# A transformer block planned by its own scheduler: fillers by a running count, later loads of the last weights, other shares of the softmax, and a direct key projection

## The chip, the cores and the metric

The kernel runs on one core of a Trainium2 chip. The core has TensorE for matrix products (PE in the profile, its weight loads PEld), VectorE (DVE), ScalarE (ACT), GpSimd (POOL) and SyncE (SP), whose queue issues nearly all transfers here. Matrix products land in PSUM, eight banks of 128 partitions by 512 floats. The metric is the device time of one execution in microseconds. The time before is 812.66 us, the median of three runs of 808.64 to 812.86.

## The reference

One block of a transformer with adaptive layer norm: 2048 tokens of 640 features, 32 heads of 20, and a gated feed-forward layer of width 1536 without a nonlinearity. All inputs are bf16.

```python
mod = silu(c) @ w_mod                      # six vectors of 640: sa, ca, ga, sb, cb, gb
h = layernorm(x) * (1 + ca) + sa
q, k, v = split(h @ wqkv)                  # 32 heads of 20
p = softmax(q @ k.T * 20 ** -0.5)          # 32 x 2048 x 2048
x = x + ga * ((p @ v) @ wo)
h = layernorm(x) * (1 + cb) + sb
x = x + gb * (((h @ w_gate) * (h @ w_up)) @ w_down)
```

## The kernel before

**How it is made.** The kernel file is a planner. It makes tasks (one or a few instructions each, with an engine, an assumed duration, dependencies, a priority and sometimes a gate), plays them through a model of the core, engine by engine, and then writes out each engine's instructions in the order that came out, with semaphore waits where one engine needs another. So the order on each queue is fixed when the program is built, and a changed number in the planner can move every instruction. At run time each engine goes through its list in order and waits where its data is late.

**Tiling.** The heads form eight sets of four; the four heads of a set sit in the four 32-row strips of the array, so that their products run side by side. The queries are cut into six chunks (`CHUNKS`): two of 512 tokens and four of 256, numbered 0 to 5. An item is one chunk and one head set, 48 in all; the last one is halved. A unit is 512 columns of scores: one head, 128 keys by 512 queries, or 256 keys by 256 queries. An item has 64 units with 512 queries, 32 with 256.

**The softmax.** Scores (line 1502) come out with keys on the partitions. Most units go in pairs to ScalarE, whose exponential (1539) writes a bf16 tile of 1024 columns into a ring `PP`; two pairs of PSUM banks take turns. The other units go in quads of four to VectorE. It builds the exponential from the bits of a scaled score: one instruction per unit turns it into an integer (1563), two passes over the quad's 2048 columns take the mantissa and the exponent (1595, 1603), and one product (1600 on VectorE, or four pieces at 1615 on GpSimd, whichever is free first in the plan) makes the first of two terms. The product with the values (2165) takes a ScalarE unit once and a quad's unit twice, once per term. `QUADS` says how many quads each head set of each chunk has. There are 104 quads, so 816 exponentials are left for ScalarE.

**Around it.** Layer norm, the projections of keys, queries and values, and the modulation vectors are made at the start and during chunk 0. A key projection of 512 tokens is either direct (`kq_round`, matmuls at 1148: one head set per round, already spread over the four strips, evicted straight into the key tile `KT`), or packed (`packed_round`, 1212: 128 features per round, evicted to `KPA`, written to memory, and read back into the strips, four reads per head set, issued at 1271). `K_DIRECT` makes head set 0 direct for all four blocks of 512 tokens; `K_ALL` lists blocks in which all sets are direct, and is empty.

When an item's products are done, its PSUM bank is transposed (1695), divided by the softmax's sum (1702, on GpSimd), transposed again into `OcT` (1711), and moved by a few small transfers into `Ocp` (1723), four or five per item. When the eight items of a chunk are there, its suffix follows: output projection with `wo` (`op`), second layer norm, transposes into h2T (1866), gate and up products with weights streamed from memory (1907), their product, and the down projection with `wd`. The suffix of one chunk is spread over the scores of the next as optional work for TensorE. The last chunk's suffix runs behind all scores, with full-width matmuls (948; 952 is the four-strip form). Its weights are loaded into buffers `stx` that take the place of dead query tiles; ten of its twelve pairs of loads go there, of which the first wait for the last scores of chunk 4 (`qdead`), and the rest for chunk 3's down projection (`first`). The others go through three rotating buffers `stg`.

**How TensorE's order is chosen.** `pick_pe` takes, at each free moment of TensorE in the plan: the next pair of scores if its banks and inputs are ready; quad units that are late; nothing, if the next scores are about to be ready (`HOLD`); optional work, if TensorE's recent activity is under `FILL_MIN`; a filler, if it is under `FILL_HARD` (0: never); a batch of value products; optional work; and last a filler, if activity is under `FILL_MIN` and nothing else is there. A filler (2498) is four matmuls of the identity into a spare bank, and its result isn't used. Activity is counted as array area over the last `HAM_W` = 3413.3 ns; the planner counts cold windows on a fixed grid and doubles its durations behind one (`roll`). `STAGE` sets such numbers anew at given items.

A load's landing in the plan is its issue, a rate, a latency, and, past 60 us, `DMA_MARGIN`.

## Time and profile before

| | |
|---|---|
| runs | 812.86, 808.64, 812.66 us |
| profiled execution | 814.7 us, span 812.9 us |
| mean granted clock of TensorE | 0.991 |
| PE busy, instructions | 796.0 us, 14867 |
| DVE busy | 685.9 us, 1337 |
| ACT busy | 767.0 us, 851 |
| POOL busy | 360.6 us, 374 |

Engine busy times are unions of instruction spans. A group's row has the line, engine and operation, what it writes and reads, the shape and count, then its busy time, the mean duration in ns, and the idle time of the engine ahead of it with what ended most of that. In the rows of a windows view each stretch has its length, each engine's busy time and count, the clock that TensorE was granted (1.00 is full speed), the share of the DMA engines, and GB/s. Chunk 0's exponentials begin at 17 us; the later chunks' begin at about 214, 401, 497, 592 and 684 us, and the last exponential ends at 780 us.

### The profile page before, as it was taken

What the parts mean: (1) busy time and instruction counts of PE and PEld (TensorE: products, weight loads), DVE (VectorE), ACT (ScalarE), POOL (GpSimd) and SP (SyncE); (2) the same over time, 40 slices, a digit from 0 to 9 for tenths busy, and PEclk for the clock granted to TensorE, in tenths of its full rate; (3) what the DMA queues carried; (4) which work ended last, traced back from release to release, by engine and by line L of the source; (5) the groups of instructions that cost most, each with busy time, mean ns of one, the idle gap of its engine ahead of it and who ended that gap; (6) DMA issues with size and microseconds to landing.
All of it is one profiled execution on the core that took longest, in us unless ns stands there. A gap on an engine that the chain in (4) does not pass through costs nothing.

```text
span 812.9 us, 34131 instructions
## 1 busy us (share of the span) xinstructions
PE 796.0 (98%) x14867; PEld 345.3 (42%) x14867; DVE 685.9 (84%) x1337; ACT 767.0 (94%) x851; POOL 360.6 (44%) x374
## 2 busy tenths in 40 slices
PE   8999999999999999999999999999999999999998
PEld 4434424332233222233343334445555555554567
DVE  7888868899999799998988878976798989799564
ACT  6899999999999799999999999999999999999941
POOL 2346344563374343444446334453546555652200
PEclk9999999999999699999999999999999999999999
DMA  9743222213241242201300232100432054444410
GB/s 298 238 121 81 59 58 65 58 33 109 73 103 34 82 114 62 49 4 46 71 17 11 49 79 56 38 23 23 97 86 54 26 118 102 98 95 97 95 36 18
DMA packets 136387, 60.49 MB, mean 74 GB/s; under 512 B 100703, under 2 KB 136239, under 8 KB 136239
## 3 DMA queue, kind: packets, MB, share of 16 engines
q1 hardware_dynamic: 135311, 57.16, 27.4%
q8 instruction: 118, 1.93, 1.1%
q10 hardware_dynamic: 928, 1.15, 0.4%
q14 instruction: 30, 0.25, 0.1%
HBM read 46.70 MB, written 8.99 MB: 69 GB/s over the span
## 4 chain that ended last, share of the span: by engine, by line
PE 49%; ACT 40%; issue 6%; DVE 3%; DMA 1%; SPq 0%; ACTq 0%; DVEq 0%
ACT PP L1539 40%; PE ps_all L1502 17%; PE ps_all L952 13%; PE ps_all L2165 11%; PE ps_all L1212 3%; PE ps_all L948 3%; DMA wm<-in_w_mod_dram 1%; DVE DB L1563 1%; PE ps_all L1109 1%; DVE DSS L1595 1%; PE ps_all L1866 1%; PE ps_all L1148 1%; DVE DSS L1603 0%; PE ps_all L2498 0%; DVE KPA L1221 0%
## 5 line engine op out<-in xcount | busy, mean ns | idle before, releaser
L1539 ACT ACTIVATE PP<-ps_all 128x1024 bf16<-128x1024 f32 x816 | 751.0, 1157 | 7.4 <-PE ps_all L1502 6.5
L1615 POOL TENSOR_TENSOR DSS<-DB,DSS 128x512 bf16<-128x512 bf16 x260 | 295.5, 1155 | 325.1 <-DVE DSS L1603 273.4
L1502 PE MATMUL ps_all<-QT,KT 32*128 32x256 bf16 (+2 forms) x3136 | 324.0, 308 | 9.5 <-ACT PP L1539 6.1
L1563 DVE TENSOR_SCALAR DB<-ps_all 128x512 int16<-128x512 f32 x416 | 277.4, 682 | 55.1 <-PE ps_all L1502 52.8
L1502 PEld LDWEIGHTS ps_all<-QT,KT 32*128 32x128 bf16 x3136 | 89.7, 92 | 239.4 <-ACT PP L1539 202.9
L2165 PE MATMUL ps_all<-PP,Vf 128*32 128x256 bf16 (+2 forms) x2520 | 165.8, 313 | 0.8 <-DVE DB L1563 0.4
L952 PE MATMUL ps_all<-h2T,stg 128*32 128x256 bf16 (+2 forms) x2272 | 122.8, 303 | 0.2 <-DVE DB L1563 0.2
L2165 PEld LDWEIGHTS ps_all<-PP,Vf 128*32 128x32 bf16 (+1 forms) x2520 | 49.6, 94 | 83.1 <-issue 76.0
L2165 PE MATMUL ps_all<-DSS,Vf 128*32 128x256 bf16 (+1 forms) x1232 | 84.6, 317 | 0.1
L1595 DVE TENSOR_SCALAR DSS<-DB 128x2048 int16<-128x2048 int16 x104 | 74.2, 713 | 0.5
L1603 DVE TENSOR_SCALAR DSS<-DB 128x2048 int16<-128x2048 int16 x104 | 72.8, 700 | 0.6 <-PE ps_all L2165 0.6
L952 PEld LDWEIGHTS ps_all<-h2T,stg 128*32 128x32 bf16 x2272 | 50.9, 96 | 28.1 <-issue 21.4
L952 PE MATMUL ps_all<-wd,hprod 128*32 128x320 bf16 (+1 forms) x1348 | 62.4, 281 | 0.0
L1702 POOL TENSOR_TENSOR OTn<-OT,invT 128x256 bf16<-128x256 f32 (+1 forms) x47 | 38.5, 820 | 53.0 <-DVE invT L1700 53.0
L1600 DVE TENSOR_TENSOR DSS<-DB,DSS 128x2048 bf16<-128x2048 bf16 x39 | 49.3, 1265 | 0.1
L2165 PEld LDWEIGHTS ps_all<-DSS,Vf 128*32 128x32 bf16 (+1 forms) x1232 | 29.5, 95 | 24.6 <-issue 14.2
L952 PEld LDWEIGHTS ps_all<-wd,hprod 128*32 128x32 bf16 x1348 | 31.1, 96 | 16.0 <-issue 10.3
L952 PE MATMUL ps_all<-wV,hT 128*32 128x160 bf16 x1280 | 37.3, 234 | 0.5 <-DVE hT L1117 0.2
L1695 DVE STREAM_TRANSPOSE OT<-ps_all 128x256 f32<-128x256 f32 (+2 forms) x49 | 25.7, 524 | 13.2 <-PE ps_all L2165 12.9
L1212 PE MATMUL ps_all<-hT,wq 128*32 128x512 bf16 x375 | 33.2, 397 | 0.0
L1212 PE MATMUL ps_all<-hT,wk 128*32 128x512 bf16 (+1 forms) x360 | 32.8, 382 | 0.2 <-DVE Vf L1301 0.2
L952 PE MATMUL ps_all<-wo,Ocp 128*32 128x320 bf16 (+1 forms) x664 | 30.7, 280 | 0.3
(131 smaller groups left out, 524.6 us busy)
## 6 DMA issues: line engine op xcount, KB each, us to landing
stg<-in_B_w_gate_dram SPq DMA_DIRECT2D x62, 160.0 KB
stg<-in_B_w_up_dram SPq DMA_DIRECT2D x62, 160.0 KB
KT<-k_rows SPq DMA_DIRECT2D x112, 32.0 KB
wm<-in_w_mod_dram SPq DMA_DIRECT2D x3, 800.0 KB
x<-in_A_x_dram SPq DMA_DIRECT2D x7, 320.0 KB
k_rows<-KPA SPq DMA_DIRECT2D x16, 128.0 KB
QT<-q_rows SPq DMA_DIRECT2D x32, 64.0 KB
wd<-in_B_w_down_dram SPq DMA_DIRECT2D x1, 1920.0 KB
```

The lines of the kernel that those rows point to most:

```text
L952: return lambda e, b: e.matmul(ps[32 * x:32 * x + 32, b, c0 + o:c0 + o + w], lhs()[:, 32 * x:32 * x + 32], rhs() if w == n else rhs()[:, o ...
L1212: f = [lambda e, b_, k=k, x=x: e.matmul(ps[x:x + min(32, w - x), b_, :], wx[:, k, r0 + x:r0 + min(x + 32, w)], hT[tc][:, k, :], tile_posit ...
L1502: ems.append(lambda e, i=i, kt=kt: e.matmul(dstf()[:, i * u.n:(i + 1) * u.n], KT[32 * u.s:32 * u.s + 32, u.j, kt * 128:(kt + 1) * 128], QT ...
L1539: return e.activation(PPs[g % 2][:, cellp["p"], 0:nu * 512], ps[:, b0:b0 + nu, :].rearrange("p b c -> p (b c)"), AFT.Exp, scale=ESCALE)
L1563: return e.tensor_scalar(DBl[st_["slot"]][:, x * 512:(x + 1) * 512], bank(cell["b"]), EBIAS, 0.0, op0=ALU.add, op1=ALU.max)
L1595: return e.tensor_scalar(DSl[st_["ss"][0]][:, :], DBl[st_["slot"]][:, :], 0x7F, 0x3F00, op0=ALU.bitwise_and, op1=ALU.bitwise_or)
L1600: return e.tensor_tensor(d, DBl[st_["slot"]][:, :].bitcast(BF16), d, ALU.mult)
L1603: return e.tensor_scalar(DSl[st_["ss"][1]][:, :], DBl[st_["slot"]][:, :], 0x7F80, 2, op0=ALU.bitwise_and, op1=ALU.bitwise_or)
L1615: return e.tensor_tensor(d, DBl[st_["slot"]][:, x * w:x * w + w].bitcast(BF16), d, ALU.mult)
L1695: t1 = Task("dve", n * 1.1 + 70, lambda e: e.transpose(OT[:, 0:n], ps[:, item_info[it]["bank"], 0:n].rearrange("p (b q r) -> p b r q", q=3 ...
L1702: f3 = lambda e: e.tensor_tensor(OTn[:, 0:n].rearrange("p (b c r) -> p b r c", c=32, r=2), OT[:, 0:n].rearrange("p (b r c) -> p b r c", c= ...
L2165: ems.append(lambda e, i=i, kt=kt, stt=stt, stp=stp: e.matmul(ps[32 * s:32 * s + mc, bk, 0:u.n], Vf[:, (kt * H + 4 * u.j + s) * VW:(kt * H ...
```

## The change

The planner's numbers and rules change at these places.

- `roll` and `activity` keep four windows, staggered by a quarter, in place of one. Any of them under `HAM_MIN` makes the plan cold; only the first clears it.
- `FILL_HARD` is 3000 in place of 0, and the filler's test stands ahead of the optional work at low activity.
- The loads of the last chunk's weights into `stx` wait, beside what they waited for, for the transfers of chunk 4's attention outputs into `Ocp` (`oc_ready`). The plan's size of these and of the streamed weight loads (each 160 KB) goes from `2 * 128 * KD * 128 * 2` bytes to `int(STG_B * 128 * KD * 128 * 2)` with `STG_B` = 0.95, that is from 327,680 to 155,648.
- `QUADS` of chunks 2 and 3.
- `K_ALL` is `(0,)`: head sets 1 to 7 of the first 512 keys are projected by direct rounds; the five packed rounds of that block go.
- `END3` is 1: the division for the last head set of chunks 0 to 4 goes from GpSimd to VectorE.
- `DMA_MARGIN` is 500 in place of 1000.
- The transposes into h2T wait for the gate and up products that last read that buffer (for `first` in chunk 4); their evictions did so before.
- `STAGE` has other numbers for most items.

```diff
-DMA_MARGIN = 1000.0
+DMA_MARGIN = 500.0
...
     def roll(self, t):
-        w = int(t // HAM_W)
-        while self.ham_w < w:
-            self.cold = self.ham_act < HAM_MIN
-            if self.cold:
-                self.ncold += 1
-            self.ham_act = 0.0
-            self.ham_w += 1
+        for i in range(4):
+            w = int((t - i * HAM_W / 4) // HAM_W)
+            while self.ham_w[i] < w:
+                low = self.ham_act[i] < HAM_MIN
+                if low:
+                    self.ncold += 1
+                if i == 0 or low:
+                    self.cold = low
+                self.ham_act[i] = 0.0
+                self.ham_w[i] += 1
...
-QUADS = (..., (2, 1, 2, 1, 2, 1, 2, 1), (2, 1, 2, 1, 2, 1, 2, 1), (2, 2, 1, 2, 2, 2, 1, 2), ...)
+QUADS = (..., (2, 2, 1, 2, 2, 2, 1, 2), (2, 2, 1, 2, 2, 2, 1, 2), (2, 2, 1, 2, 2, 2, 1, 2), ...)
...
-K_ALL = ()
+K_ALL = (0,)
...
-FILL_HARD = 0.0
+FILL_HARD = 3000.0
...
-ENDP, END3, P_POW = 0.4, 0, -1.0
+STG_B = 0.95
+ENDP, END3, P_POW = 0.4, 1, -1.0
...
-            r = Round(mms, list(t_xn2), after, pr(True), gate=gate(n), name=f"h2T{ci}.{k}")
+            r = Round(mms, t_xn2 + (first if alt else bd.get("h2T", [])), after, pr(True), gate=gate(n),
+                      name=f"h2T{ci}.{k}")
...
-                t = dma("sp", 2 * 128 * KD * 128 * 2, f, sfx_done["qdead"] if use_x and fc < nsq else first if use_x else kp_use if ci == 0 else [], prio=16 + ci + .01 * fc,
+                t = dma("sp", int(STG_B * 128 * KD * 128 * 2), f,
+                        (sfx_done["qdead"] if fc < nsq else first) + oc_ready[(NC - 2, CHUNKS[-2][1] // 128 - 1)] if use_x else
+                        kp_use if ci == 0 else [], prio=16 + ci + .01 * fc,
...
+        if sc.recent(t) < FILL_HARD and t > 20000 and do_fill(t):
+            return True
         if sc.recent(t) < FILL_MIN and ring() >= RINGLOW and pick_x(t, True):
             return True
-        if sc.recent(t) < FILL_HARD and t > 20000 and do_fill(t):
-            return True
```

73 lines of the change are left out of this document (40 added, 33 removed).

## The prediction

> **What bounds the kernel now.** I read the page's first parts, then its costliest groups.
>
> ```profile
> span 812.9 us, 34131 instructions
> PE 796.0 (98%) x14867; PEld 345.3 (42%) x14867; DVE 685.9 (84%) x1337; ACT 767.0 (94%) x851; POOL 360.6 (44%) x374
> ...
> ACT  6899999999999799999999999999999999999941
> ...
> PEclk9999999999999699999999999999999999999999
> ...
> L1539 ACT ACTIVATE PP<-ps_all 128x1024 bf16<-128x1024 f32 x816 | 751.0, 1157 | 7.4 <-PE ps_all L1502 6.5
> ```
>
> ACT's row is full from the third slice to the third last, but for one; TensorE's 98% is partly the modelled ends of pipelined matmuls. Nearly all of ACT is one line, the exponential over two score units: 751.0 / 816 = 0.920 us each. So the span is three stretches: a head until ACT is full, 816 exponentials end to end, and a tail. The windows view and the groups of one stretch say how full:
>
> ```profile
> 20.00:100.00 80.00, 77.91 (x1414) 32.90 (x1416) 69.59 (x152) 76.31 (x85) 37.35 (x45) 1.00 0.45 128
> 260.00:280.00 20.00, 19.42 (x153) 4.67 (x153) 15.16 (x26) 15.54 (x17) 8.29 (x8) 0.66 0.06 16
> 300.00:320.00 20.00, 19.91 (x282) 5.95 (x274) 20.00 (x37) 20.00 (x23) 8.01 (x8) 1.00 0.24 55
> 395.00:490.00 95.00, 93.39 (x1788) 38.11 (x1788) 79.96 (x148) 94.94 (x104) 44.20 (x48) 1.00 0.16 38
> 490.00:587.00 97.00, 96.80 (x2146) 46.56 (x2142) 76.69 (x144) 97.00 (x107) 44.00 (x46) 1.00 0.20 49
> 587.00:680.00 93.00, 92.20 (x2253) 49.27 (x2252) 83.44 (x166) 92.88 (x102) 50.49 (x51) 1.00 0.31 71
> ...
> L1539 ACT ACTIVATE PP<-ps_all 128x1024 bf16<-128x1024 f32 x210 | 193.3, 1132 | 0.1
> ```
>
> Columns: stretch, length, busy time of PE, its weight loads, DVE, ACT and POOL (each with its count), granted clock, DMA share, GB/s. ACT lacks 80 - 76.31 = 3.7 us before 100 us, lacks 4.5 us in the slice where the clock is 0.66, and lacks nothing in chunks 2 to 4 (395 to 680). The last row is ACT's group from 400 to 592: 0.1 us idle. There only fewer exponentials can help, and retuned stage settings cannot.
>
> **The change part by part.**
>
> *More quads on VectorE.* The tuple for chunks 2 and 3 goes from 2,1,2,1,2,1,2,1 (12) to 2,2,1,2,2,2,1,2 (14): four sets gain a quad, two lose one. So the net is four quads in all, though the change is named for six: 104 become 108. A quad is four units and an exponential takes two: 8 exponentials fewer, 8 x 0.920 = 7.4 us off ACT. VectorE pays, by these rows:
>
> ```profile
> L1563 DVE TENSOR_SCALAR DB<-ps_all 128x512 int16<-128x512 f32 x416 | 277.4, 682 | 55.1 <-PE ps_all L1502 52.8
> ...
> L1603 DVE TENSOR_SCALAR DSS<-DB 128x2048 int16<-128x2048 int16 x104 | 72.8, 700 | 0.6 <-PE ps_all L2165 0.6
> L1600 DVE TENSOR_TENSOR DSS<-DB,DSS 128x2048 bf16<-128x2048 bf16 x39 | 49.3, 1265 | 0.1
> L1615 POOL TENSOR_TENSOR DSS<-DB,DSS 128x512 bf16<-128x512 bf16 x260 | 295.5, 1155 | 325.1 <-DVE DSS L1603 273.4
> ```
>
> Per quad 4 x 0.682 + 2 x 0.700 (the two passes have one shape) = 4.1 us, and the product either on VectorE (1.27, 5.4 in all) or on POOL (4 x 1.155 = 4.6; POOL is half idle). Chunk 3: 76.7 + 2 x 5.4 = 87.5 of 97 - 3.7. Chunk 2 is tight: 80.0 + 10.8 = 90.8 of 95 - 3.7 = 91.3. Chunk 4 already has the new pattern, with ACT at 92.88 of 93, and from 300 to 320 VectorE is busy 20.00 of 20 with ACT still full. So I book VectorE's extra 17 to 22 us at nothing; if chunk 2 overflows, its share of the gain is lost (a rival below). TensorE's second product pass for 16 units has the same cover.
>
> *Fillers by a running count.* The planner now keeps four staggered 3.4 us windows, and puts in a filler as soon as its count of the last window is under 3000 (a full window is 3413 ns x 2.37, about 8090), ahead of optional work. What this is about:
>
> ```profile
> 263.00:264.00 1.00, 1.00 (x6) 0.18 (x6) 1.00 (x3) 1.00 (x2) 0.56 (x1) 0.50 0.03 8
> ...
> 259.60:263.00 3.40, 2.82 (x25) 1.05 (x23) 3.40 (x7) 3.40 (x5) 1.92 (x2) 1.00 0.13 32
> 200.20:203.60 3.40, 2.30 (x28) 0.64 (x26) 3.40 (x6) 2.86 (x4) 0.18 (x1) 1.00 0.52 154
> 306.00:309.40 3.40, 3.40 (x57) 1.15 (x53) 3.40 (x9) 3.40 (x5) 0.00 (x0) 1.00 0.10 25
> L1539 ACT ACTIVATE PP<-ps_all 128x1024 bf16<-128x1024 f32 x11 | 11.1, 1056 | 4.4 <-PE ps_all L1502 4.4
> L2498 PE MATMUL ps_all<-ident x128: 379/379/391, 219.5 to 742.8; 128*32 128x512 bf16 x128
> ```
>
> The granted clock halves at 263, and by the slice's 0.66 stays there some 20 x 0.34 / 0.5 = 13.6 us, after 3.4 us with 25 matmuls where an ordinary stretch has 57. The stretch at 200 was as thin (28) and kept its clock: it depends on how the count falls. While the clock is low the exponentials wait for scores (group of 262.9 to 276.7). The price: 17 exponentials in that 20 us slice instead of 23, 6 x 0.92 = 5.5 us; the idle time alone is 4.5. I take 5.5, as each lone exponential also runs longer than its 0.92 in a stream. Without it this execution would be 814.7 - 5.5 = 809.2, close to the lowest timed run, 808.64. A filler is four matmuls of 0.38 us side by side; before had 32. Costs are in the cover row below.
>
> [...]
>
> *Last weights behind the attention outputs.* These rows are from the timeline, tiles, groups by form, DMA issues, and the chain in order of time.
>
> ```profile
> 687.27 0.31 DVE L1711 STREAM_TRANSPOSE OcT<-OTn 128x128 f32<-128x128 f32 x1
> 692.56 2.99 SPq L1723 DMA_DIRECT2D Ocp<-OcT  x4
> 702.37 0.53 PE L952 MATMUL ps_all<-wo,Ocp 128*32 128x320 bf16 x12
> L952 PE MATMUL ps_all<-h2Tt,stg x544: 219/272/283, 725.5 to 774.9; 128*32 128x256 bf16 x140, 128*32 128x128 bf16 x42
> L952 PE MATMUL ps_all<-wd,hprodt x192: 298/299/310, 781.8 to 789.9; 128*32 128x320 bf16 x192
> L952 PE MATMUL ps_all<-wd,hprodt 128*32 128x320 bf16 x192 | 7.3, 300 | 0.0
> x<-in_A_x_dram ACTq DMA_DIRECT2D x1, 320.0 KB, 2.9
> 783.49 1.35 DVE L1856 TENSOR_SCALAR h2Tc<-ps_all,mcol 128x128 bf16<-128x128 bf16 x5
> 775.95 2.26 ACT PP L1539 x2
> ...
> 783.56 4.05 PE ps_all L952 x116
> ...
> 790.15 20.07 PE ps_all L948 x300
> ```
>
> Chunk 4's last output is transposed by 687.6 but issued at 692.6, behind weight loads on SP, and first used at 702.4. Issued at once, with 3.0 us for the four issues and 2.9 to land (the one transfer whose landing the page times, an estimate here), they would be there at 693.5: the projection could start 8.9 us sooner. What it feeds ends late: all 48 down-projection steps of chunk 4 (192 matmuls, 8 us) run after the last exponential and push chunk 5's final 20.07 us to 790.15. Gate and up of chunk 4 take 725.5 to 774.9, 49.4 us for 12 x 10 steps of 256 columns; 8.9 us is 18% of that, 5,530 columns, or 36% of the down projection's 48 x 320 = 15,360: 0.36 x 7.3 us busy = 2.6 us off the tail from this alone. Ends: nothing, and 790.15 - (783.49 + 1.35) = 5.3 us, when chunk 5's first half is ready and nothing is left over. The moved loads have until 790 and start near 693: covered.
>
> *First 512 keys projected direct.* K_ALL = (0,) is the first token block, all head sets 1 to 7 (the name says head set 0). Five packed rounds become seven direct ones:
>
> ```profile
> L1212 PE MATMUL ps_all<-hT,wk 128*32 128x512 bf16 (+1 forms) x360 | 32.8, 382 | 0.2 <-DVE Vf L1301 0.2
> ```
>
> Matmuls: 140 for 90, or +50 x 32.8 / 360 = +4.6 us of TensorE at the spread-out price; two evictions more (0.68 each); 28 reads (7 sets by 4 strips) and 6 writes go from SP. It lies in the head, where ACT lacks 3.7 us: ends -3.7 and +4.6, and I take 0.
>
> *The planner's idea of loads.* For the streamed weights the plan's size goes from 327,680 bytes, twice the true 160 KB, to 155,648, and the margin from 1.0 to 0.5 us. At the plan's 240 bytes per ns and 0.0015 ns per byte that is a landing 0.72 + 0.26 + 0.5 = 1.5 us sooner, 3.1 us after the issue instead of 4.6. Nothing in the chip changes but the order: rounds may be placed sooner.
>
> ```profile
> SPq L1907 <- PE ps_all L952: 95.9, 46, 4.1
> stg<-in_B_w_gate_dram SPq DMA_DIRECT2D x62, 160.0 KB
> 678.64 0.53 SPq L1907 DMA_DIRECT2D stg<-in_B_w_up_dram  x1
> 680.50:681.00 0.50, 0.50 (x26) 0.29 (x14) 0.50 (x1) 0.50 (x2) 0.00 (x0) 1.00 0.75 167
> ...
> PEld ps_all L973 <- DMA wm<-in_w_mod_dram: 1.7, 2, 1.1
> ...
> PEld ps_all L1502 <- ACT PP L1539: 202.9, 642, 1.4
> ```
>
> SP waits for TensorE to free a buffer (95.9 us), so landing time is in each buffer's cycle. The pair whose second load is issued at 678.64 has ended its traffic by 681, 2.4 us later, so 3.1 still holds in a quiet queue, and no PE row waits for a transfer but one at the start. Chunk 4 turns its three buffers (12 - 3) / 3 = 3 times: up to 4.4 us sooner, which I add to the 8.9: 13.3 / 49.4 = 27%, 8,270 columns, 54% of 15,360, and 0.54 x 7.3 = 3.9 us off the tail in place of 2.6, still inside 0 to 5.3.
>
> *The rest.* Five normalisations go from POOL to VectorE, the transposes of h2T carry one wait more (for a buffer that their evictions waited for already), and some forty stage settings change: beside a full ACT, 0. Fillers too: the score loads wait 642 times for ACT, 0.32 us on average (last row), so a filler of 0.38 us costs at most some hundredths; with that cover gone, 0.38 each.
>
> **Sum**, against this execution's own 814.7 (span 812.9): 814.7 - 7.4 - 5.5 - 3.9 = 797.9. The median of the runs is 812.66 and the lowest 808.64; two runs near 812.7 look like this one and the lowest like one whose clock held, from which the sum is 808.64 - 11.3 = 797.3. I predict 798.
>
> **The rivals.** (1) *The clock still falls once.* For: the stretch at 200 shows that a thin stretch is decided by where it falls, and the planner's count is not the chip's. Against: the new count looks at every moment, and four phases are kept. 814.7 - 7.4 - 3.9 = 803.4. (2) *The quads do not pay.* For: chunk 2's 90.8 of 91.3 us, and 55.1 us in which VectorE waited for scores, which it cannot make up. Then late quads hold the products back and ACT waits instead: no 7.4, 814.7 - 5.5 - 3.9 = 805.3; with the tail unmoved as well, 809.2. Against: chunk 4 and 300 to 320. (3) *Slower: TensorE stalls on weights that the plan counts too early.* Its queue is in order, so behind a gate or up round that waits stand the next scores, and ACT behind them. In a dense stretch the plan now moves a 160 KB load in 0.65 us; the half microsecond from 680.5 moved 167 GB/s, 0.98 us for as much. Price: up to 1.5 us for each of the 62 streamed pairs, 93 us at worst. It decides from (816.7 - 798) / 1.5 = 13 pairs fully late. Against: no such wait now, and the 0.7 us between 2.4 and 3.1. At some 20 pairs, 798 + 30 = 828.
>
> **How the numbers follow.** A measurement of this kernel can tell about 0.5%, 4 us, from no change: 808.6 to 816.7. Chances: forecast 0.60, rival 1 0.15, rival 2 0.13, rival 3 0.12. Faster: 0.60 + 0.15 + half of rival 2 = 0.81; same: the other half and the mild part of rival 3, 0.09; slower 0.10. Range: low end with the full tail and the head's idle time gained, 814.7 - 7.4 - 5.5 - 5.3 - 3.7 = 793; high end with the clock fall kept, no tail gain and the direct keys' full price nearly, 814.7 - 7.4 + 3.7 = 811.
>
> **What would show it.** Exponentials x808 at 0.92; no stretch under 1.00 in the clock row; ACT full from 100 us on; VectorE's group L1563 x432; chunk 4's first projection near 693 and part of its down projection ahead of the last exponential; 28 key reads fewer. Wrong: ACT waiting for scores in chunk 2, PE rows that wait for DMA, or a clock under 1.00.

## The result and the profile after

The changed kernel takes 807.97 us, the median of 20 runs (803.90 to 815.22). The kernel before took 811.37 us beside it, also over 20 runs (808.19 to 817.06). The ratio is 0.9954, with a 95% interval of 0.9934 to 0.9974. So the change is worth about 3.7 us. Here and below the medians and ranges hold every run, and the ratios leave out three runs (one of e2_space, two of e7_q3) that were over 1.5% above the fastest of their kernel. I had forecast 798 us, and a change of 16.8 us in the profiled execution (814.7 to 797.9). The profiled execution of the changed kernel took 810.71 us, 4.0 less.

The lines of the file have moved: 1539 is now 1550 (exponentials), 1502 is 1513 (scores), 1563 is 1574, 1595 is 1606, 1603 is 1614, 1600 is 1611, 1615 is 1626 (quads), 1702 is 1713 (the division), 1907 is 1919 (streamed weights), 952 and 948 are 963 and 959. These lines of the page after answer to those shown of before:

```profile
span 808.9 us, 34210 instructions
...
PE 791.2 (98%) x14913; PEld 346.7 (43%) x14913; DVE 700.8 (87%) x1368; ACT 761.1 (94%) x843; POOL 375.6 (46%) x385
...
PEclk9999999998999999999999999999999999999999
...
L1550 ACT ACTIVATE PP<-ps_all 128x1024 bf16<-128x1024 f32 x808 | 745.4, 1109 | 11.6 <-PE ps_all L1513 10.6
...
L1574 DVE TENSOR_SCALAR DB<-ps_all 128x512 int16<-128x512 f32 x432 | 288.4, 683 | 46.4 <-PE ps_all L1513 43.7
...
KT<-k_rows SPq DMA_DIRECT2D x84, 32.0 KB, 1.7
```

The counted things came as forecast: 808 exponentials at 745.4 / 808 = 0.92 us, 432 quad units on VectorE, 84 key reads in place of 112. But ScalarE's exponentials now stand idle for 11.6 us, ended by scores; before it was 7.4. The stretches, from the starts of the exponentials at each chunk's border, say where. The third column is the mended kernel e6_end_wait of the experiments below, which has the changed kernel's order of instructions but for ten loads:

| us | before | after | e6_end_wait |
|---|---|---|---|
| head, to the first exponential | 17.0 | 16.2 | 16.2 |
| chunk 0 | 197.1 | 200.1 | 196.8 |
| chunk 1 | 186.8 | 183.6 | 181.7 |
| chunk 2 | 95.8 | 92.7 | 92.6 |
| chunk 3 | 95.4 | 92.2 | 92.0 |
| chunk 4 | 92.0 | 92.2 | 92.4 |
| chunk 5, to the end of its last exponential | 96.0 | 100.5 | 95.9 |
| tail behind it | 32.9 | 31.4 | 31.4 |
| span | 812.9 | 808.9 | 799.0 |

Chunks 2 and 3 and the tail gave something; chunk 1 lost its fall of the clock and got a smaller one; chunks 0 and 5 lost 3.0 and 4.5 us. The windows view of the changed kernel at the three places (columns as before: length, PE, its weight loads, DVE, ACT, POOL, granted clock, DMA share, GB/s):

```profile
194.24:197.65 3.41, 2.56 (x25) 0.70 (x21) 3.41 (x6) 3.22 (x4) 2.22 (x2) 1.00 0.44 158
197.65:201.06 3.41, 3.41 (x25) 0.51 (x22) 3.19 (x7) 2.05 (x2) 1.44 (x2) 0.50 0.06 16
341.01:344.42 3.41, 2.11 (x27) 0.65 (x27) 3.40 (x7) 3.04 (x4) 1.25 (x2) 1.00 0.23 53
344.42:347.84 3.42, 3.42 (x31) 0.76 (x33) 2.06 (x4) 2.27 (x4) 1.15 (x1) 0.50 0.04 12
740.37:743.78 3.41, 1.39 (x36) 0.79 (x36) 0.76 (x3) 0.62 (x2) 2.51 (x3) 1.00 0.84 181
743.78:747.20 3.42, 3.42 (x56) 1.51 (x52) 2.14 (x4) 2.66 (x3) 0.00 (x0) 0.50 0.51 109
```

The rows come in pairs: 3.41 us with few matmuls for its time (25, 27, 36), and behind each a clock of 0.50. The clock had fallen once in the profile before, for 13.65 us; it now fell three times, for 6.83, 3.41 and 3.41 us. That is 13.65 us again, and the mean clock is 0.991 in both. What made the stretches thin is in the timeline (a row has its start, its length, the engine, and in brackets the idle time before it with its releaser):

```profile
194.64 0.65 DVE L1606 TENSOR_SCALAR DSS<-DB 128x2048 int16<-128x2048 int16 x1
194.80 1.40 POOL L1713 TENSOR_TENSOR OTn<-OT,invT 128x512 bf16<-128x512 f32 x1 [3.31 <-DVE invT L1711]
...
195.21 1.54 DVE L1614 TENSOR_SCALAR DSS<-DB 128x2048 int16<-128x2048 int16 x1
...
197.40 0.10 PEld L1513 LDWEIGHTS ps_all<-QT,KT 32*128 32x128 bf16 x3 [1.15 <-DVE DB L1574]
197.40 0.41 PE L1513 MATMUL ps_all<-QT,KT 32*128 32x512 bf16 x3 [0.85 <-DVE DB L1574]
...
339.77 2.08 DVE L1496 TENSOR_TENSOR wd<-wd,gab 128x640 bf16<-128x640 bf16 x3
339.94 1.17 POOL L1713 TENSOR_TENSOR OTn<-OT,invT 128x512 bf16<-128x512 f32 x1 [5.53 <-DVE invT L1711]
...
343.20 0.39 PE L1513 MATMUL ps_all<-QT,KT 32*128 32x512 bf16 x3 [1.01 <-DVE DB L1574]
```

At 194.80 GpSimd starts the division of a 512-query item, as soon as its input is there. VectorE's pass at 195.21 then takes 1.54 us where its twin at 194.64 took 0.65. The quad's units after it are late, so TensorE's scores wait 0.85 us for their banks (their weight loads, PEld, wait 1.15). At 340 it is the same with three small products and a wait of 1.01 us. The third place is another matter; SyncE's queue first, and then TensorE and ScalarE:

```profile
730.58 1.81 SPq L1919 DMA_DIRECT2D stg<-in_B_w_up_dram  x1
732.43 0.53 SPq L1919 DMA_DIRECT2D stx<-in_B_w_gate_dram  x1
733.00 0.56 SPq L1919 DMA_DIRECT2D stx<-in_B_w_up_dram  x1
733.60 3.88 SPq L1734 DMA_DIRECT2D Ocp<-OcT  x5
737.52 0.48 SPq L1919 DMA_DIRECT2D stg<-in_B_w_gate_dram  x1
738.05 0.52 SPq L1919 DMA_DIRECT2D stg<-in_B_w_up_dram  x1
...
742.39 0.62 PE L963 MATMUL ps_all<-h2Tt,stg 128*32 128x256 bf16 x16 [2.71 <-DMA stg<-in_B_w_up_dram]
...
743.37 2.12 ACT L1550 ACTIVATE PP<-ps_all 128x1024 bf16<-128x1024 f32 x2 [2.79 <-PE ps_all L1513]
```

Chunk 4's gate and up product waits 2.71 us for its weights, the scores behind it in TensorE's queue wait too, and ScalarE stands for 2.79 us. The pair had been issued from 737.52 to 738.57, behind stx loads and five small Ocp transfers, and its second load was there 3.8 us after its issue ended (742.39), where the plan has 3.1.

### The profile page after: what moved, and what is told of

It reads as the page before. It is cut to its first block, busy times and chain, and to the rows that moved or that the text cites. A ratio compares the mean times of both kernels' runs of the same rounds, so it can differ in the third digit from the quotient of the medians.

```text
span 808.9 us, 34210 instructions
## 1 busy us (share of the span) xinstructions
PE 791.2 (98%) x14913; PEld 346.7 (43%) x14913; DVE 700.8 (87%) x1368; ACT 761.1 (94%) x843; POOL 375.6 (46%) x385
## 3 DMA queue, kind: packets, MB, share of 16 engines
q10 hardware_dynamic: 928, 1.15, 0.4%
## 4 chain that ended last, share of the span: by engine, by line
PE 65%; ACT 20%; DVE 8%; issue 4%; DMA 2%; SPq 2%; ACTq 0%
PE ps_all L1513 22%; ACT PP L1550 20%; PE ps_all L963 19%; PE ps_all L2179 16%; PE ps_all L959 3%; PE ps_all L1223 3%; DVE DB L1574 3%; DMA stg<-in_B_w_up_dram 1%; PE ps_all L1159 1%; DVE DSS L1614 1%; SPq L1734 1%; DMA wm<-in_w_mod_dram 1%; DVE DSS L1606 1%; SPq L1919 1%; PE ps_all L1120 0%
## 5 line engine op out<-in xcount | busy, mean ns | idle before, releaser
L1550 ACT ACTIVATE PP<-ps_all 128x1024 bf16<-128x1024 f32 x808 | 745.4, 1109 | 11.6 <-PE ps_all L1513 10.6
L1626 POOL TENSOR_TENSOR DSS<-DB,DSS 128x512 bf16<-128x512 bf16 x276 | 314.0, 1158 | 321.4 <-DVE DSS L1614 246.3
L1574 DVE TENSOR_SCALAR DB<-ps_all 128x512 int16<-128x512 f32 x432 | 288.4, 683 | 46.4 <-PE ps_all L1513 43.7
L2179 PE MATMUL ps_all<-PP,Vf 128*32 128x256 bf16 (+4 forms) x2488 | 164.0, 312 | 0.0
L2179 PE MATMUL ps_all<-DSS,Vf 128*32 128x256 bf16 (+3 forms) x1296 | 88.0, 312 | 0.1
L1606 DVE TENSOR_SCALAR DSS<-DB 128x2048 int16<-128x2048 int16 x108 | 75.0, 695 | 1.6 <-PE ps_all L2179 1.2
L1614 DVE TENSOR_SCALAR DSS<-DB 128x2048 int16<-128x2048 int16 x108 | 75.1, 695 | 0.0
L1713 POOL TENSOR_TENSOR OTn<-OT,invT 128x256 bf16<-128x256 f32 (+1 forms) x42 | 33.9, 808 | 43.1 <-DVE invT L1711 43.0
L2179 PEld LDWEIGHTS ps_all<-DSS,Vf 128*32 128x32 bf16 (+1 forms) x1296 | 32.8, 95 | 22.1 <-issue 12.9
L963 PE MATMUL ps_all<-wV,hT 128*32 128x160 bf16 x1280 | 39.1, 234 | 0.6 <-issue 0.2
L963 PEld LDWEIGHTS ps_all<-wV,hT 128*32 128x32 bf16 x1280 | 24.1, 96 | 15.3 <-issue 9.0
```

What stands on the lines that cost most here:

```text
L963: return lambda e, b: e.matmul(ps[32 * x:32 * x + 32, b, c0 + o:c0 + o + w], lhs()[:, 32 * x:32 * x + 32], rhs() if w == n else rhs()[:, o ...
L1550: return e.activation(PPs[g % 2][:, cellp["p"], 0:nu * 512], ps[:, b0:b0 + nu, :].rearrange("p b c -> p (b c)"), AFT.Exp, scale=ESCALE)
L1574: return e.tensor_scalar(DBl[st_["slot"]][:, x * 512:(x + 1) * 512], bank(cell["b"]), EBIAS, 0.0, op0=ALU.add, op1=ALU.max)
L1606: return e.tensor_scalar(DSl[st_["ss"][0]][:, :], DBl[st_["slot"]][:, :], 0x7F, 0x3F00, op0=ALU.bitwise_and, op1=ALU.bitwise_or)
L1614: return e.tensor_scalar(DSl[st_["ss"][1]][:, :], DBl[st_["slot"]][:, :], 0x7F80, 2, op0=ALU.bitwise_and, op1=ALU.bitwise_or)
L1626: return e.tensor_tensor(d, DBl[st_["slot"]][:, x * w:x * w + w].bitcast(BF16), d, ALU.mult)
```

## The experiments

Theory: the forecast's parts were there, and three local losses ate them. Two come from GpSimd starting a division earlier than the plan has it, which holds VectorE and thins TensorE's work until the clock falls; one from weights that the plan counts as landed before they are. Rivals: the fillers do nothing; the clock falls by TensorE's own order; the loads would be late in any order; the quads or the tail were worth less than booked.

In some expectations "count of work" stands for the columns of each matmul times the share of the array it uses, summed over 3.41 us by the starts of the matmul rows. For a full stretch the plan counts about 8090, and the expectation of e1_no_fill says 8192; the fullest 3.41 us of the two profiles, before and after, hold 8320. It is my own sum over rows, not a row of a view.

**e1_no_fill: are the fillers worth anything?** The changed kernel has nine fillers behind the start, seven from 430 to 435 us; before had 32. Here they are one column wide.

```diff
+        if t > 20000:
+            task.emits = [lambda e: e.matmul(ps[0:32, b_, 0:1], ident[:, 0:32], ident[:, 0:1],
+                                             tile_position=(0, 0), skip_group_check=True)]
```

> The changed kernel with its nine later fillers (seven at 430 to 435 us, two at 699 us) cut to matmuls of one column; order and waits stay. Measure of work: columns times share of the array that a matmul takes, summed over 3.41 us; 8192 is a full stretch. In the two profiles so far the clock was halved behind stretches of 3.41 us that held 2260 to 2900 of it and not behind those that held 3140 or more. Theory (the clock follows this count, and the fillers hold it): the least stretch near 432 us falls from 3412 to 1792, so the clock is halved for at least 3.4 us near 436 us, the exponentials behind it start 1.5 to 2 us later, and the kernel takes about 810 us instead of 808. Rival (the fillers do nothing that counts): clock 1.00 from 425 to 450 us, time within 0.5 us of the changed kernel's.

Measured: 810.45 us (12 runs, 808.50 to 814.63), ratio to the kernel before 0.9991 (0.9969 to 1.0013). The windows view of the place:

```profile
429.39:432.80 3.41, 2.51 (x50) 1.12 (x44) 3.30 (x9) 3.41 (x5) 3.33 (x7) 1.00 0.01 2
432.80:436.21 3.41, 3.10 (x39) 1.15 (x39) 3.10 (x8) 3.41 (x4) 1.63 (x2) 0.50 0.00 0
```

Without them the clock falls, and stayed low for 13.65 us from 432.8, not for one stretch of 3.41; chunk 2 lasts 96.4 us in place of 92.7. All 12 runs have a mean clock of 0.992 or less, and 16 of the changed kernel's 20 runs have more. So the fillers do what they are for, where the plan sees a thin stretch: 2.5 us in the medians, 3.0 by the two ratios.

**e3_wait: is GpSimd's early start the cause of the falls at 197 and 344?** The planner already keeps GpSimd's operations apart from VectorE's passes, but in its own time only. One condition less makes it a real wait, on the VectorE pass that the plan put before; the schedule stays the same.

```diff
-            elif task.lk == 2 and self.lk_last is not None and self.lk_last.done > self.t - 3000.0:
+            elif self.lk_last is not None and self.lk_last.done > self.t - 3000.0:
```

> The changed kernel with one more wait: each of GpSimd's SBUF operations (the normalisation L1713 above all) waits for the VectorE pass that the schedule put ahead of it; order and buffers stay. Theory (the thin stretches at 196 and 342 us come from GpSimd starting early, 194.80 us, beside a VectorE pass that then takes 1.54 us instead of 0.68): that pass takes 0.7 us again, TensorE's waits for VectorE of 0.85 and 1.01 us go, the clock stays at 1.00 at 198 to 204 and 344 to 348 us, chunk 0 is 2.5 to 3.2 us and chunk 1 about 2 us shorter, the kernel takes about 803 us instead of 808. Rival (the stretches are thin by TensorE's own order, GpSimd has no part): both falls stay, time within 0.7 us. Rival 2 (GpSimd is late with the normalisation): the passes are short but transposes and later products wait, and the time rises by up to 3 us.

Measured: 805.64 us (6 runs, 802.75 to 806.62), ratio 0.9914 (0.9882 to 0.9945). The timeline of e3_wait:

```profile
195.20 0.69 DVE L1614 TENSOR_SCALAR DSS<-DB 128x2048 int16<-128x2048 int16 x1
...
195.80 1.88 DVE L1574 TENSOR_SCALAR DB<-ps_all 128x512 int16<-128x512 f32 x3
...
195.97 1.05 POOL L1713 TENSOR_TENSOR OTn<-OT,invT 128x512 bf16<-128x512 f32 x1 [4.48 <-DVE DSS L1614]
...
196.54 0.24 PEld L1513 LDWEIGHTS ps_all<-QT,KT 32*128 32x128 bf16 x3 [0.29 <-DVE DB L1574]
```

The pass takes 0.69 us again, the division follows it, the wait of the scores' weight loads is down from 1.15 to 0.29 us, and the profile has no low clock before 736. Chunks 0 and 1 last 196.8 and 181.6 us: 3.3 and 2.0 less, where 2.5 to 3.2 and about 2 were expected. The median gained 2.3 us where 5 was expected, since the wait for weights was in this profile as well (3.0 us at 734, with 6.83 us of half clock behind it), and since the two falls are not in every run of the changed kernel: its 20 runs have mean clocks from 1.000 to 0.987.

The profiles of e1_no_fill, e2_space, e12_old_load and e8_tail tell the two parts of the loss from each other. They have the same order of instructions here without the wait, and the same pass takes 1.54 us, but the clock stayed whole at both places. In them chunk 0 lasts 197.5 to 198.4 us and chunk 1 182.2 to 182.3. So the held-up VectorE alone costs 0.7 to 1.7 us in chunk 0 and 0.6 to 0.7 in chunk 1, and the rest of the 3.3 and 2.0 us is the fallen clock. GpSimd's early start makes the stretch thin in every one of these profiles; whether the clock then falls is left to the execution. Without the wait it fell near 197 us in two of the seven profiles with this order, and near 344 in three; with the wait in none of four.

**e2_space and e4_both: the order of the stx loads.** In e2_space the last ten stx loads go one behind each pair of stg loads; e4_both is that with the wait of e3_wait.

```diff
+    spread(sc)
     nw = emit_program(nc, sc)
...
+def spread(sc):
+    late = [t for t in sc.all if t.name == "stx" and t.start > 710e3]
+    pairs = [t for t in sc.all if t.name == "stg1" and t.start > 716e3]
+    for t, p in zip(late, pairs):
+        sc.all.remove(t)
+        sc.all.insert(sc.all.index(p) + 1, t)
```

> The changed kernel with the last ten stx loads (chunk 5's gate and up weights) issued one behind each pair of stg loads of chunk 4, instead of ten ahead of or among the first three pairs; nothing else moves. Theory (TensorE's wait of 2.71 us at 739.7 us comes from SP, which issues eight stx loads at 0.45 to 1.0 us each ahead of the pair): the wait goes, with it the halved clock at 743.8 us; the last exponential ends 4 to 4.7 us earlier, the kernel takes about 804 us instead of 808. Rival 1 (a pair of 160 KB simply lands too late for double buffers, whoever is ahead of it): a wait of 1 us or more stays at one of the pairs of chunk 4, gain under 1.5 us. Rival 2 (the stx loads now land too late for chunk 5's gate and up projection behind the last exponential): the stall is gone but the stretch behind the last exponential grows from 31.4 us by what is gained.

> e2_space and e3_wait together. Theory (three local losses make the difference between forecast and result, and they add): 808.0 less 4 to 4.7 less 4.5 to 5.4 is 798 to 799.5 us, clock 1.00 through to the end, ratio to the kernel before 0.983 to 0.986. Rival (with these stretches mended the clock falls at the next thinnest, for example the 3.41 us from 186.3 us with 2176 or near 437 us with 3284): 801 to 804 us and at least one halved stretch in the profile.

Measured: e2_space 806.47 us (12 runs, 803.36 to 816.86), ratio 0.9933 (0.9903 to 0.9963); e4_both 806.11 us (9 runs, 802.43 to 813.63), 0.9921 (0.9885 to 0.9958). Both miss in the median; the five runs of e2_space at a mean clock of 1.000 take 803.4 to 804.2 us, near the 804 expected. The waits view of e2_space from 725 to 770 us (us in total, times, longest), and then its row in the timeline:

```profile
PE ps_all L963 <- DMA stg<-in_B_w_up_dram: 2.6, 3, 1.8
```

```profile
759.47 0.62 PE L963 MATMUL ps_all<-h2Tt,stg 128*32 128x256 bf16 x8 [1.84 <-DMA stg<-in_B_w_up_dram]
```

The wait only moved, to a pair behind the next Ocp group with stx loads still among the pairs, and the clock was halved behind it for 13.65 us (20.48 us in e4_both). The rival that a pair beside anything else is late had it here.

**e5_end and e6_end_wait: the stx loads behind everything.** Now the ten loads go behind SyncE's last transfer before the last exponential, so that they start near 762 us.

```diff
     late = [t for t in sc.all if t.name == "stx" and t.start > 710e3]
-    pairs = [t for t in sc.all if t.name == "stg1" and t.start > 716e3]
-    for t, p in zip(late, pairs):
-        sc.all.remove(t)
-        sc.all.insert(sc.all.index(p) + 1, t)
+    last = [t for t in sc.all if t.eng == "sp" and t.start < 760e3][-1]
+    for t in late:
+        sc.all.remove(t)
+    at = sc.all.index(last) + 1
+    sc.all[at:at] = late
```

> The changed kernel with the last ten stx loads (chunk 5's gate and up weights) issued behind everything else that SP has before the last exponential (near 766 us), so that no load but chunk 4's own stg pairs stands in SP's queue beside chunk 4's gate and up projection; nothing else moves. In e2_space the wait had moved from 740 us to 757.8 us (1.64 to 1.8 us, behind five Ocp transfers that took SP 3.3 us, with an stx load between the pairs). Theory (SP's queue and the transfers beside it make the pair late, and the stx loads are what is too much): no TensorE wait for stg above 1 us from 725 to 770 us, the last exponential ends some 4 us before 777.5, runs at full clock take about 801 us instead of 804, the median is 804 to 805.5. Rival 1 (five Ocp transfers alone make a pair late): a wait of 1.5 us or more stays behind one Ocp group. Rival 2 (stx is late for its use, which starts at 786 us): the stretch behind the last exponential grows beyond 32 us.

> e5_end with e3_wait's extra wait. e3_wait measured 805.6 us, with a TensorE wait of 3 us at 734 us and 6.8 us of halved clock behind it in its profile. Theory (what is left is that wait): without it 800 to 801.5 us, full-clock runs about 799, ratio to the kernel before 0.985 to 0.988. Rival (a thinner end of chunk 5 drops the clock as in e4_both, 20 us of half clock from 761 us): 803 us or more with a halved stretch behind 755 us.

Measured: e5_end 805.10 us (12 runs, 803.12 to 814.52), ratio 0.9921 (0.9890 to 0.9951). Its waits view from 725 to 770 us has no row for stg, and chunk 5 lasts 95.9 us in place of 100.5; its own profile was lost to the first cause (a low clock from 197.5 to 221.4). Its four runs at a mean clock of 1.000 take 803.1 to 803.6 us, not the 801 that were expected. With the wait, e6_end_wait takes 801.06 us (6 runs, 800.36 to 803.24), ratio 0.9869 (0.9832 to 0.9906), below the changed kernel's interval. Five of its six runs have a mean clock of 1.000, where the changed kernel has three of 20. From the page of e6_end_wait, and then from its chain in order of time (start, length, what):

```profile
span 799.0 us, 34214 instructions
...
PEclk9999999999999999999999999999999999999999
```

```profile
753.62 2.00 ACT PP L1550 x3
...
768.09 1.74 PE ps_all L959 x12
...
772.31 3.10 PE ps_all L963 x88
776.32 20.07 PE ps_all L959 x300
```

The three local losses are gone, and chunk 5's final 20.07 us begin at 776.32 where they began at 786.17. Since nothing but one wait and the place of ten loads differs from the changed kernel, the losses are shown to be these two causes, each with the clock that falls behind it. The table above adds up: 3.3 + 1.9 + 4.6 = 9.8 of the 9.9 us between the profiled executions, 810.71 and 800.84.

**e12_old_load: does the plan's idea of a load make the wait?** For chunks 4 and 5 the plan counts a gate or up load as before the change, 327,680 bytes and a margin of 1.0 us.

```diff
+            if task.name == "wl":
+                task.done += 500.0
...
-                t = dma("sp", int(STG_B * 128 * KD * 128 * 2), f,
+                t = dma("sp", int((2.0 if ci >= NC - 2 else STG_B) * 128 * KD * 128 * 2), f,
...
+                        name="wl" if ci >= NC - 2 else "")
```

> The changed kernel with the plan's old idea of a load (327,680 bytes and a margin of 1.0 us) for the gate and up weights of chunks 4 and 5 alone; the schedule is the same up to some 720 us, and behind that the plan puts the fourth gate and up round of chunk 4 6.9 us later and the last 17.8 us later, with 12 fillers more. Theory (the new idea of a load lets the plan place these rounds sooner than their weights land on the chip, and the wait at 740 us is the price): TensorE waits for no stg load by more than 1 us behind 725 us, the clock does not halve there, and the last exponential ends about 4 us sooner than in a run of the changed kernel with that wait; but less of chunk 4's gate, up and down products is done by then, and the stretch behind the last exponential grows from 31.4 us by 2 to 5 us, so the median is 806 to 809 us. Rival (the order of the stx loads alone makes the wait, whatever the plan thinks of a landing): a wait of 1.5 us or more stays near 740 us.

Measured: 808.26 us (12 runs, 807.65 to 811.82), ratio 0.9953 (0.9928 to 0.9979). No row for stg in its waits view behind 720 us, clock 1.00 up to the end of the span, chunk 5 in 95.9 us. And the end of its chain, in which lines 963 and 959 of the changed kernel are 965 and 961:

```profile
778.98 5.95 PE ps_all L965 x172
784.93 19.18 PE ps_all L961 x284
```

The last exponential ends at 770.4 in a span of 806.7, so the tail is 36.3 us, 4.9 longer. As expected: the shorter landing in the plan pays with work done sooner and costs a wait on the chip, and the two cancel. Placing the stx loads elsewhere (e6_end_wait) keeps the one without the other.

**e8_tail: would earlier work of chunk 4 shorten the tail?** The matmuls of chunk 4's down projection behind the last exponential are cut to one column. That part of the computation is left out.

```diff
+    for t in sc.all:
+        if t.name.startswith("dn4") and t.start > last.start + last.dur:
+            t.emits = [lambda e, f=f: f(OneColumn(e)) for f in t.emits]
```

> The changed kernel with the matmuls of chunk 4's down projection that stand behind the last exponential cut to one column (144 of them; that part of the computation is left out); order and waits stay. Theory (they only fill the time in which VectorE and GpSimd normalise chunk 5's second tile, so it matters little how early chunk 4's work is): the stretch behind the last exponential shortens by under 0.8 us from 31.4. Rival (they stand in TensorE's queue ahead of the first gate matmul of chunk 5, whose first half of h2T is evicted by 783.5 while the matmul starts at 786.1, so earlier projections would have paid as forecast): it shortens by 2 to 3.5 us.

Measured: 810.93 us (10 runs, 805.99 to 814.72), ratio 0.9987 (0.9957 to 1.0017). The end of the changed kernel's chain, then that of e8_tail, and a row of e8_tail's windows view:

```profile
780.30 1.47 PE ps_all L963 x40
782.16 3.10 PE ps_all L963 x88
786.17 20.07 PE ps_all L959 x300
```

```profile
777.76 3.35 issue
...
783.13 22.19 PE ps_all L959 x300
```

```profile
783.13:787.54 4.41, 4.41 (x43) 4.41 (x44) 1.75 (x5) 0.67 (x2) 0.00 (x0) 0.50 0.11 37
```

The last exponential ends at 777.48 and 774.65, so the final block starts 8.7 us behind it in the one and 8.5 in the other: the 144 matmuls stood in time that was waiting anyway. With them cut TensorE was busy for 5.23 of the 8.48 us from 774.65 to 783.13, and the clock was halved from 780.7 to 787.5 (the last row); the final block took 2.1 us longer (22.19 for 20.07), and the whole tail is 33.3 us instead of 31.4, so neither statement holds as it stands. That half clock began 2.4 us before the block, so it may hide up to 1.2 us of a gain; between 0.2 and 1.4 us, an estimate, is what the cut is worth to the start of the block, and the 5.3 us that I had taken as the end of the range is out. In e12_old_load, where all 192 of these matmuls and 80 of gate and up stand behind the last exponential, the block goes on 14.5 us behind it: the cover has an end.

**e7_q3: what is an exponential worth?** Chunk 3 has its old quads.

```diff
-QUADS = (..., (2, 2, 1, 2, 2, 2, 1, 2), (2, 2, 1, 2, 2, 2, 1, 2), ...)
+QUADS = (..., (2, 2, 1, 2, 2, 2, 1, 2), (2, 1, 2, 1, 2, 1, 2, 1), ...)
```

> The changed kernel with chunk 3's quads as before the change (12 instead of 14 on VectorE), so four exponentials more on ScalarE in that chunk; the schedule is the same up to chunk 3 and another one behind it. Theory (ScalarE's stream sets the pace there, each exponential is 0.92 us less what VectorE's extra work costs): chunk 3, exponentials 520 to 628, lasts 3.0 to 3.7 us longer than its 95.8 us. Rival (VectorE is the bound there already and two quads more only move the load): under 1.5 us longer. The total is not expected to show it alone, since the schedule behind is a new one.

Chunk 3 lies between 492.55 and 584.75 us in the changed kernel and between 490.22 and 585.75 here (the expectation numbered its exponentials otherwise: the chunk has 100 in the one and 104 in the other). A row of the windows view of each, the changed kernel first:

```profile
492.55:584.75 92.20, 91.92 (x2052) 43.95 (x2048) 82.85 (x157) 92.16 (x101) 46.33 (x46) 1.00 0.16 39
```

```profile
490.22:585.75 95.53, 95.20 (x2114) 45.63 (x2110) 77.09 (x148) 95.50 (x105) 41.88 (x44) 1.00 0.20 48
```

Four exponentials more take 3.3 us, 0.83 each, with ScalarE full in both. (The 95.8 us of the expectation belong to another count; chunk 3 lasts 92.2 in the changed kernel.) The total, 817.71 us (10 runs, 814.01 to 827.02; ratio 1.0055, 1.0024 to 1.0086), has another schedule behind chunk 3, with a wait for stg of 3.0 us and two falls of the clock in the profile; so it tells only how much a new order of the work can cost.

**e9_before_wait: would the wait have helped the kernel before?** The edit of e3_wait, in the kernel before.

> The kernel before, with the extra wait of e3_wait alone. In its trace the thin stretch of 260 to 273 us has no VectorE pass held up (its passes there take 0.68 and 1.21 us), so it comes from the order of the work itself. Theory (the wait mends only stretches where GpSimd starts early, and the changed kernel had two of those in new places): the halved stretch near 263 us stays in runs as before and the median is 809.5 to 811.5 us, ratio 0.997 to 1.000. Rival (the wait is a general gain that the kernel before would have had as well): as in the changed kernel, 2 us or more in the median, ratio below 0.9965.

Measured: 809.27 us (12 runs, 807.22 to 815.58), beside 810.61; ratio 0.9981 (0.9955 to 1.0007). The ratio is where the theory had it, though the interval does not shut the rival out: at a mean clock of 1.000 its four runs have a median of 807.5 us beside 808.75 of three of the kernel before. Its profile had the clock whole at 263 and halved for 3.41 us at 68, so the fall at 263, which the theory had staying, is not in every run of that schedule either. Chunk 1 lasts 181.5 us there and 186.8 in the profile before, where the clock fell: 5.3 us.

**e10_half_fill: how much of a filler is needed?** e6_end_wait with the nine fillers 256 columns wide.

```diff
+            half = ident[:].unsqueeze(1).to_broadcast([128, 2, 128])
+            task.emits = [lambda e, x=x: e.matmul(
+                ps[32 * x:32 * x + 32, b_, 0:256].rearrange("p (a b) -> p a b", a=2), ident[:, 32 * x:32 * x + 32], half,
+                tile_position=(0, 32 * x), skip_group_check=True) for x in range(4)]
```

> e6_end_wait with the nine later fillers half as wide (256 columns instead of 512). Least count of work in 3.41 us near 427 us: 3284 with whole fillers, 1792 without, about 2650 with half. Theory (halved clock behind a count below some 2900, read from the profiles): half fillers do not hold the clock, most runs have at least one halved stretch, and the median is 1.5 to 3 us above e6_end_wait's 801.1. Rival (any matmul in the gap holds it, or the limit lies below 2600): clock 1.00 in nearly all runs and a median within 0.6 us of 801.1.

Measured: 801.09 us (6 runs, 800.26 to 804.46), ratio 0.9867 (0.9835 to 0.9900), the same as e6_end_wait. The rival had the outcome: the least count over any 3.41 us near 427 us came out at 2624, and the profile has no low clock. That doesn't show a limit below 2600. The changes of the clock keep a grid of 3.41 us within an execution (last section), and on this one's grid the thin place is cut in two, so that the lowest stretch there holds 3264. Two of the six runs have a mean clock below 1.000 (0.994 and 0.998), of e6_end_wait one, so six runs do not tell half a filler from a whole one.

**e11_no_k: the direct keys undone.** `K_ALL` is empty again, and the schedule a new one from the head on.

```diff
-K_ALL = (0,)
+K_ALL = ()
```

> The changed kernel with head set 0's keys through k_rows as before the change (112 key reads instead of 84); the schedule behind the head is a new one, so the total tells little (its fillers, waits and order differ). Theory (the direct keys are worth nothing that counts, since the first exponential waits for other work): the first 100 exponentials start within 0.7 us of where they start in the changed kernel (first at 16.2, hundredth near 105 us). Rival (the reads bound the head): they start 1.5 us or more later; or, were the direct path the dearer one, as much earlier.

The windows view of the exponentials' line alone from 16 to 116 us (length, ScalarE's busy time and count, clock, DMA share, GB/s), the changed kernel first:

```profile
16.00:116.00 100.00, 93.22 (x101) 1.00 0.40 112
```

```profile
16.00:116.00 100.00, 92.22 (x100) 1.00 0.41 120
```

The first exponential starts at 16.15 us in the one and 16.13 in the other. 101 exponentials have begun in the stretch in the one, 100 in the other; the hundred-and-first starts at 115.2 and 116.6 us (the expectation's 105 was a slip). A difference of 1.4 us lies between the two cases, and the new order around it may make it. The total is 816.09 us (10 runs, 812.39 to 822.45), ratio 1.0064 (1.0033 to 1.0095), and is the price of another order of everything.

## Why the prediction was wrong

Against the sum, 814.7 - 7.4 - 5.5 - 3.9 + 0 + 0 = 797.9, the profiled execution after took 810.7, 12.8 more. That the median of 807.97 us lies inside the stated 793 to 811 is no merit of the sum: the high end has one fall kept, no gain in the tail and most of the direct keys' price, and what happened was something else.

- **Fillers by a running count, -5.5: the step that failed.** Its price was right: the 95 runs of the kernel before that stand beside the experiments have a median of 808.75 us at a mean clock of 1.000 (16 runs) and of 814.21 at 0.992 (9 runs), 5.5 us. That it would be gone was wrong: both profiled executions have 13.65 us at half clock, so the term gave nothing. The fillers hold the stretches that the plan counts as thin (e1_no_fill: without them 13.65 us at half clock from 432.8). The stretches that fell had waits which the plan doesn't have, and no filler stood there. The rival for this (the clock still falls) had the right outcome, for the reason that I gave against myself in it: what the planner counted is not what ran, for the waits of 0.85, 1.01 and 2.71 us are not in the plan; I gave it 0.15 and priced one fall, where there were three. With that step, the forecast also compared an execution of before with a fallen clock with one of after with a whole one; at a mean clock of 1.000 the two kernels took 808.75 (median of 16 runs) and 803.9 to 806.5 (3 of the 20, median 805.2).
- **The rest, 0: failed as well.** I booked the new order of some forty settings at nothing beside a full ScalarE. The new order put two divisions on GpSimd beside VectorE passes, 3.3 us in chunk 0 and 1.9 in chunk 1 with the falls behind them, by the difference to e6_end_wait. Which of the change's numbers made this order, no run shows. ScalarE is full only as long as nothing thins TensorE's scores: even with a whole clock these two places cost 0.7 to 1.7 and 0.6 to 0.7 us (e3_wait).
- **The planner's idea of loads: rival 3's cause, once.** One pair, not 13. I had priced a pair at 1.5 us and asked how many it takes to be slower than before; a single one cost 4.6 us in chunk 5, 2.7 us of wait and then half clock behind it. The sum had no term for it. I compared one landing in a quiet queue, 2.4 us, with the plan's 3.1, and didn't set SyncE's issue times against the plan's 0.40 us each: here one load took 1.81 and five Ocp transfers 3.88. e12_old_load shows that the sooner rounds make the wait; e6_end_wait that the loads' order alone can take it away.
- **The tail, -3.9: too much; it gave 1.4 (32.9 to 31.4).** The first half held and more: chunk 4's output projection starts at 687.95, 14.4 us sooner. The second half failed: gate and up begin at 724.66 in place of 725.5, behind chunk 3's down projection, so the sooner projection bought no sooner gate and up. They were faster (43.4 us for 49.4), and 48 of the 192 down-projection matmuls moved ahead of the last exponential. What was left to push is cover only (e8_tail).
- **More quads, -7.4: 6.3 (3.1 in chunk 2, 3.2 in chunk 3).** The mechanism was right (e7_q3 tests it for chunk 3; chunk 2's part rests on the two profiles). An exponential less is worth 0.78 us here and 0.83 in e7_q3, not its whole 0.92. That VectorE would hold in chunk 2 was right too: by ScalarE's group it stands idle for 0.3 us in the 196 exponentials from 404 to 584 us.
- **Direct keys, 0:** the first exponential started 0.8 us sooner (16.15 for 16.97), within the ends -3.7 and +4.6. That is not shown to be theirs: without them it starts at 16.13 (e11_no_k), and at 17.03 in e2_space with them. By the hundred-and-first, e11_no_k leaves 0 to 1.4.

The sum with the measured terms is 814.7 - 6.3 - 1.4 - 0.8 - 5.5 = 800.7, and e6_end_wait's profiled execution took 800.84; 9.9 us of local losses lie on top of it in the profiled execution after. By the runs at a mean clock of 1.000 (medians 805.2 and 800.84) an estimated 4.4 of the 9.9 us are the waits themselves, which the forecast had at nothing, and the other 5.5 are the falls of the clock, which it had as gone. So of the 12.8 us 5.5 are the filler term, 4.4 the waits, 2.5 the tail and 1.1 the quads, less 0.8 at the head, to a rounding. Of the list of what would show each step right, the clock row and "ScalarE full from 100 us" came out against me, and the row that I had named as a sign of error, TensorE waiting for a transfer, was there.

## What to carry to other kernels

A schedule that is written out by a planner meets the chip only where the planner's model has the effect: if it keeps two engines apart in its own time, make that a wait in the program; here one line took the median from 805.10 to 801.06 us (e5_end, e6_end_wait). When a load's assumed landing is shortened, compare the time that the issuing queue takes for what stands ahead of it (here 3.9 us for five small transfers), not only the landing of one. Before crediting a gain for a clock that no longer falls, look over the timed runs for those in which it didn't fall before: that much of the gain is in the old kernel already.

## What the runs showed of the hardware

- The halved clock comes in pieces of 3.41 us: 3.41, 6.83, 10.24, 13.65, 20.48 and 23.89 us in these profiles. The whole clock between two falls does too: in the changed kernel 139.94 us from 204.48 to 344.42 and 395.95 from 347.83 to 743.78 are 41 and 116 pieces of 3.413 us, so the changes keep one grid in an execution. By the two medians above a piece costs an estimated 5.5 / 4 = 1.4 us, as a mean clock of 0.992 is four pieces at half clock (13.65 / 2 / 812.9 = 0.008). Whether a thin stretch makes it fall differs between executions of one schedule: e2_space and e5_end have the same order of instructions up to some 720 us, and one page has the clock whole to 759 us, the other low from 197.5 to 221.4 and once more at 351. By my count of work on that grid, the whole-clock stretches ahead of the falls hold 320 to 2968 over all these profiles; behind the first 20 us seven stretches with 2176 to 2944 kept the clock, five of them near 186 to 191 us, and none with 3072 or more lost it. So the count alone doesn't decide (2968 lost the clock, 2176 kept it); that the place where the grid cuts a thin stretch decides part of it is my reading, and no run tests it.

The clock rows of e2_space and of e5_end:

```profile
PEclk9999999999999999999999999999999999999789
```

```profile
PEclk9999999998599999999999999999999999999999
```

- A stretch need not be idle for the clock to fall behind it: TensorE was busy 2.56 and 2.11 of the 3.41 us before the changed kernel's falls at 197.65 and 344.42, and 2.82 of the 3.40 us before the fall at 263 in the kernel before. Ahead of the one at 743.78 it was busy 1.39 of 3.41.
- In e5_end the low clock lasted seven pieces (23.89 us from 197.5) where the changed kernel, with the same work, recovered after two (6.83 us from 197.65). That scores at half speed come late, and that what waits for them thins the next stretch, is my reading of one profile, not shown by a run.
- A VectorE pass that started beside a GpSimd operation on SBUF took 1.54 us in the changed kernel (195.21) and 0.69 without GpSimd beside it (e3_wait, 195.20), with GpSimd at work in the first 0.99 us of the 1.54 (195.21 to 196.20). The pass ahead of it, under way when GpSimd started, took 0.65 us (194.64), and the units that read PSUM keep 0.63 us each (1.88 us for three in e3_wait's timeline at 195.80, with GpSimd at work from 195.97). What held the pass up the traces don't show.
- A load of 160 KB takes SyncE mostly 0.37 to 0.53 us to issue (medians in the changed kernel: 0.42 for 62 gate loads into stg, 0.53 for 62 up loads). Single ones took more: 1.81 us where ten stand together (730.58 in the changed kernel), and 1.65 where two pairs do (729.32 in e6_end_wait). What makes these long the runs don't show.
